# A fused linear-attention and token-mixing kernel: w spread by TensorE, decay by exponentials, tables and weights taken at other times, all orders searched anew

## The chip, the cores and the metric

The kernel runs on one core of one Trainium2 chip. The metric is device time in microseconds (us) of one execution. A verdict of faster or slower needs 2%. A run counts as slow when it is over 1.5% above the fastest run of the same kernel, and only fast runs are compared. Profiles are of one execution each, and their span is some 1.7 us shorter than the timed run's figure.

Engines in the profile: PE is TensorE (PEld its weight loads), DVE VectorE, ACT ScalarE, POOL GpSimd, SP SyncE, which here issues loads and stores. "L929" is a line of the kernel's file. A trailing q (SPq) is an engine's instruction queue.

## The reference, cut to what matters

```python
def _attn_ref(r, k, v, w, u):                 # r, k, v: 4 x 8 x 768 x 48; w, u: 8 x 48
    for t in range(S):
        cur = einsum('bhd,bhe->bhde', u * kt, vt)
        y[:, :, t] = einsum('bhd,bhde->bhe', rt, state + cur)
        state = w * state + einsum('bhd,bhe->bhde', kt, vt)

def _moe_ref(x, w_theta, w_tok_r, w_tok_i, w_ch):   # x: 4 x 768 x 384, the y of above
    theta = x @ w_theta
    zr, zi = x * cos(theta), x * sin(theta)
    u = x + w_tok_r @ zr + w_tok_i @ zi             # over the tokens
    return u + maximum(u @ w_ch, 0)
```

The kernel takes 256 tokens at a time (a pair of chunks of 128). The decay w becomes powers of w: r is scaled by w^t and k by w^-t, so that the recurrence turns into matrix products. The powers are `exp(t * ln w)`, made once on ScalarE, and everything else waits for them.

## The kernel before

The kernel is a list of tasks. Each task has an engine, a planned duration, the names that it reads (`rd`) and writes (`wr`), and a priority. A planner puts them in order with a table of tuned priorities, and they are then emitted in that order. Two things of it matter below. First, dependencies come from the order in which tasks are *added*:

```python
def add(self, opts, fn, rd=(), wr=(), prio=0.0, ...):
    # ... cut
    for k in rd:
        if k in self.writer:
            deps.add(self.writer[k])        # read after write
    for k in wr:
        if k in self.writer:
            deps.add(self.writer[k])
        deps.update(self.readers.get(k, ()))  # write after read
```

A task that reads a name before any writer of it has been added doesn't wait for the writer. It is the writer, added later, that waits for it. Second, where the planner expects TensorE to idle, it puts filler: two matmuls of zeros each, 100 such pairs.

```python
def warm(e):
    for _ in range(2):
        nc.tensor.matmul(bank("warm")[:, :C], zeros, zeros, start=True, stop=True, ...)
```

The start that the change rewrites:

```python
# w to all 128 partitions in one load, ln of it, six tables of powers
nc.scalar.dma_start(out=w_all, in_=...)               # the row repeated 128 times
P.add({ACT: act_op(HD)}, lambda e: nc.scalar.activation(
    bank("w")[:, :HD], w_all, Act.Ln), rd=["table", "w_all"], ...)
# ... six Exp: wpow x2, wpinvj x2, wpinv x2
P.add({ACT: (1280, 0)}, lambda e: nc.scalar.preload_act_table_set("trig_and_small"),
      rd=[(t, n) for t in ("wpow", "wpinv", "wpinvj") for n in range(2)],
      wr=["tables done"], prio=-186, name="trig")
# ... wup = w and u by partition, transposed on TensorE
def power(e):                                          # w ** 256, by squaring
    for i in range(REF.bit_length() - 1):
        nc.vector.tensor_mul(wR, *[wR if i else wup[:, :HP]] * 2)
P.add({DVE: (8 * 75, 142)}, power, rd=["wup"], wr=["wR"], prio=-100)
# ... wS = wR spread, on VectorE
```

Of the kernel before, what the change touches and what calls it, by code (L numbers as in the profile page):

```python
# [27 lines left out]
    0: (-1896, 4), 1: (-2763, 4), 2: (-4995, 2), 3: (-3601, 2), 4: (-2443, 2), 5: (-1397, 2), 6:  # L28
    (-3159, 16), 7: (-2942, 16), 8: (-3463, 8), 9: (-3515, 2), 10: (-1403, 8), 11: (-2193, 2), 12:
    (-3435, 8), 13: (-681, 8), 14: (-937, 8), 15: (2071, 8), 16: (1103, 4), 17: (-619, 4), 18:  # L30
    (-926, 4), 19: (-4791, 4), 20: (-2748, 4), 21: (-3667, 4), 22: (-771, 4), 23: (-754, 4), 24:
    (-1822, 1), 25: (-1861, 2), 26: (2175, 2), 27: (-4, 2), 28: (-2, 2), 129: (-1155, 16), 130:
    (-4315, 4), 131: (-1061, 16), 132: (-2753, 4), 133: (-2053, 16), 134: (-1978, 16), 135:
    (-3238, 16), 136: (-3891, 8), 137: (-4590, 1), 138: (-3333, 4), 139: (-4189, 8), 140: (-5295,
    1), 141: (-4754, 4), 142: (-3834, 12), 143: (-2711, 1), 144: (-2685, 4), 145: (-4467, 1), 146:
    (-4690, 2), 147: (-2495, 1), 148: (-4276, 2), 149: (-842, 2), 150: (-2017, 1), 151: (-2622,
    2), 152: (-1180, 8), 153: (-3428, 1), 154: (-4163, 4), 155: (-3120, 1), 156: (-5116, 2), 157:
    (-94, 1), 158: (1961, 1), 159: (1825, 2), 160: (-1058, 1), 161: (215, 2), 162: (263, 1), 163:
    (1029, 4), 164: (-378, 4), 165: (-96, 2), 166: (858, 8), 167: (-1833, 16), 168: (-1750, 16),
    169: (-1556, 16), 170: (-621, 10), 171: (-655, 1), 172: (3105, 4), 173: (2182, 2), 174: (2622,  # L40
    1), 175: (-569, 4), 176: (1579, 12), 177: (2292, 1), 178: (233, 4), 179: (1643, 1), 180: (339,
    2), 181: (809, 1), 182: (4670, 2), 183: (1450, 2), 184: (1167, 1), 185: (2345, 6), 186: (-114,
    8), 187: (1042, 1), 188: (2242, 4), 189: (-581, 1), 190: (532, 2), 191: (2385, 1), 192: (1695,
    1), 193: (822, 2), 194: (-853, 1), 195: (-1349, 2), 196: (-240, 1), 197: (2674, 4), 198: (789,
    4), 199: (-2387, 2), 200: (-74, 8), 201: (-1619, 16), 202: (-1567, 16), 203: (-1103, 16), 204:
    (-1330, 8), 205: (-400, 1), 206: (-29, 4), 207: (1699, 2), 208: (2535, 1), 209: (793, 4), 210:
    (2521, 12), 211: (3075, 1), 212: (392, 6), 213: (1782, 1), 214: (958, 2), 215: (2441, 1), 216:
    (1197, 2), 217: (924, 2), 218: (-921, 1), 219: (861, 2), 220: (1383, 8), 221: (1810, 1), 222:
    (1772, 2), 223: (-1328, 1), 224: (-1335, 1), 225: (-330, 2), 226: (-3469, 1), 227: (358, 2),
    228: (-3341, 1), 229: (-1638, 4), 230: (-1248, 4), 231: (-1246, 2), 232: (-588, 8), 233:  # L50
    (-1217, 16), 234: (-835, 4), 235: (-2791, 1), 236: (-486, 4), 237: (-1096, 16), 238: (-635,
    4), 239: (-2397, 1), 240: (-273, 6), 241: (-1017, 16), 242: (-621, 8), 243: (-2952, 1), 244:
    (-1704, 6), 245: (-994, 16), 246: (-2200, 12), 247: (-3308, 1), 248: (-816, 2), 249: (-829,
    16), 250: (-2428, 4), 251: (-3835, 1), 252: (-2176, 4), 253: (-681, 16), 254: (-2655, 4), 255:
    (-4721, 1), 256: (-1118, 2), 257: (-1043, 16), 258: (-1015, 16), 259: (-935, 16), 260: (-1828,
    16), 261: (-1011, 16), 262: (793, 8), 263: (909, 1), 264: (-33, 4), 265: (1341, 8), 266: (-71,
    1), 267: (380, 2), 268: (229, 12), 269: (-1257, 1), 270: (-362, 2), 271: (-3268, 1), 272:
    (265, 2), 273: (601, 2), 274: (-1105, 1), 275: (251, 4), 276: (-1692, 8), 277: (784, 1), 278:
    (69, 4), 279: (-1813, 1), 280: (-632, 2), 281: (-2190, 1), 282: (-3799, 1), 283: (-1835, 2),
    284: (-3289, 1), 285: (-2993, 4), 286: (-2547, 1), 287: (-1541, 4), 288: (-2225, 4), 289:  # L60
    (-2974, 2), 290: (-4026, 8), 291: (-887, 16), 292: (-1726, 8), 293: (-3616, 1), 294: (669, 6),
    295: (-588, 16), 296: (-1662, 12), 297: (-1938, 1), 298: (-362, 2), 299: (-639, 16), 300:
    (1192, 8), 301: (-3068, 1), 302: (13, 4), 303: (-1228, 16), 304: (-351, 12), 305: (-2932, 1),
    306: (-1642, 2), 307: (-871, 16), 308: (-323, 12), 309: (-4673, 1), 310: (-2831, 4), 311:
    (-664, 16), 312: (-2302, 4), 313: (-4826, 1), 314: (178, 2), 315: (-633, 16), 316: (-1135, 4),
    317: (-385, 16), 318: (-1248, 4), 319: (-789, 16), 320: (-655, 16), 321: (-631, 16), 322:
    (-481, 16), 323: (-815, 16), 324: (400, 8), 325: (-1810, 1), 326: (-1751, 4), 327: (-3166, 8),
    328: (-2789, 1), 329: (-3217, 6), 330: (-4693, 12), 331: (-3955, 1), 332: (-5497, 2), 333:
    (-4006, 1), 334: (-2820, 2), 335: (-900, 2), 336: (-1916, 1), 337: (-1250, 2), 338: (-1478,
    8), 339: (-3240, 1), 340: (-3478, 2), 341: (-3355, 1), 342: (-1715, 2), 343: (-1485, 1), 344:  # L70
    (-3363, 1), 345: (-1582, 2), 346: (-2081, 1), 347: (160, 2), 348: (-2004, 1), 349: (-689, 4),
    350: (-420, 4), 351: (-1725, 2), 352: (-1969, 8), 353: (-1341, 16), 354: (-1303, 16), 355:
    (-1238, 16), 356: (-1289, 16), 357: (-1210, 16), 358: (-3381, 8), 359: (-2762, 1), 360:
    (-2524, 4), 361: (-2830, 8), 362: (-3386, 1), 363: (-2897, 4), 364: (-4632, 4), 365: (-2013,
    1), 366: (-849, 2), 367: (-523, 1), 368: (1139, 2), 369: (-3189, 2), 370: (-3513, 1), 371:
    (-136, 2), 372: (-267, 8), 373: (1251, 1), 374: (-1229, 6), 375: (2164, 1), 376: (942, 1),
    377: (-3734, 2), 378: (472, 1), 379: (-932, 6), 380: (-2042, 1), 381: (1568, 4), 382: (-1352,
    4), 383: (244, 2), 384: (591, 8), 385: (-1168, 1), 386: (961, 1), 387: (677, 1), 388: (1888,
    1), 389: (-234, 1), 390: (-667, 1), 391: (-2365, 2), 392: (777, 1), 393: (-998, 1), 394:
    (-1886, 1), 395: (-3010, 1), 396: (-2471, 1), 397: (-3265, 1), 398: (-2463, 2), 399: (-1584,  # L80
    1), 400: (5, 4), 401: (-611, 1), 402: (-2652, 2), 404: (1045, 1), 405: (-2138, 1), 406:
    (-1323, 1), 407: (-2353, 1), 408: (-3333, 1), 409: (-1347, 1), 410: (-466, 2), 411: (1541, 1),
    412: (-902, 1), 413: (-1133, 1), 414: (-530, 1), 415: (1936, 1), 416: (-134, 1), 417: (768,
    2), 418: (-2718, 1), 419: (1200, 4), 420: (-1242, 1), 421: (-420, 2), 423: (-2297, 1), 424:
    (1071, 1), 425: (723, 1), 426: (2291, 1), 427: (92, 1), 428: (1298, 1), 429: (2134, 2), 430:
    (-582, 1), 431: (-1329, 1), 432: (-1371, 1), 433: (209, 1), 434: (-1462, 1), 435: (-4595, 1),
    436: (-1376, 2), 437: (-219, 1), 438: (-565, 6), 439: (-2142, 1), 440: (795, 2), 442: (-1207,
    16), 443: (-1191, 16), 444: (-970, 16), 445: (-929, 16), 446: (-1092, 16), 447: (556, 8), 448:
    (1415, 1), 449: (924, 4), 450: (829, 8), 451: (-178, 1), 452: (-1305, 6), 453: (682, 8), 454:
    (222, 1), 455: (-2254, 2), 456: (474, 1), 457: (174, 2), 458: (-34, 2), 459: (-2544, 1), 460:  # L90
    (-914, 2), 461: (303, 8), 462: (676, 1), 463: (-391, 4), 464: (-444, 1), 465: (-2364, 2), 466:
    (-1246, 1), 467: (-515, 1), 468: (-3108, 2), 469: (373, 16), 470: (-2049, 1), 471: (-2310, 4),
    472: (-2144, 4), 473: (-4193, 2), 474: (-1119, 8), 475: (-896, 16), 476: (-1250, 16), 477:
    (-740, 16), 478: (-677, 16), 479: (-1314, 16), 480: (804, 8), 481: (764, 1), 482: (-3469, 4),
    483: (-2213, 8), 484: (-507, 1), 485: (-3583, 6), 486: (-2024, 4), 487: (-2611, 1), 488:
    (-4241, 2), 489: (-5630, 1), 490: (-4793, 2), 491: (-3160, 2), 492: (-3117, 1), 493: (-425,
    4), 494: (-941, 8), 495: (786, 1), 496: (-1076, 2), 497: (-1758, 1), 498: (-561, 2), 499:
    (-636, 1), 500: (-1124, 1), 501: (1106, 2), 502: (2312, 16), 503: (-1559, 1), 504: (-936, 4),
# [228 lines left out]
def act_op(n, psum=True, ptr=False):  # L327
    return (n / 1.2 + (50 if psum else 100) + (90 if ptr else 0), 175)
# [40 lines left out]
def build(ctx, tc, nc, r, k, v, w, u, moe_w_theta, moe_w_tok_r, moe_w_tok_i, moe_w_ch, out):  # L369
    B, H, S, D = r.shape  # L370
    HD = H * D
# [609 lines left out]
```

## Time and profile before

| | before |
|---|---|
| median of 3 timed runs | 144.17 us (144.04 to 144.65) |
| the run that was profiled | 145.99 us, span 144.3 us, mean granted clock 0.976 |
| TensorE busy | 133.4 us, 17.4 of it filler |
| table loads of ScalarE | 2 |

Note the second row: the profile was taken on a run slower than the three timed ones. This comes back below.

The prediction shows most of the lines. One view it treats as unimportant is the end. These are the DMA throughput in GB/s of before in its last 7 us (40 slices of 0.175 us), and SyncE's waits in its last 10 us (who waits at which line, for what, total us, times, longest).

```profile
GB/s 298 325 395 386 334 404 9 0 0 0 0 0 0 0 0 0 0 0 97 369 395 360 360 386 343 378 395 334 386 351 325 18 0 0 0 0 0 0 0 0
```

```profile
SPq L976 <- DMA out_dram<-fin: 1.7, 1, 1.7
```

The last stores move at over 300 GB/s and stop dead, eight slices (1.4 us) before the end. SyncE's final wait for them is 1.7 us.

### The profile page before, as it was taken

To read this page: it belongs to the slowest core of one execution; us is meant where nothing else is said; L and a number is where in the kernel's file an instruction comes from. 1 tells how busy PE (TensorE), PEld (TensorE's weight loads), DVE (VectorE), ACT (ScalarE), POOL (GpSimd) and SP (SyncE) were. 2 spreads that over 40 slices of the span, in tenths; PEclk is the share of its full clock that TensorE was granted. 3 is DMA by queue.
4 is the path that set the end of the run, shared out by engine and by line. 5 is a ranking of instruction groups with operands and counts; after the bars stand their busy time and mean duration, and the time that the engine had idled before them with its cause. 6 is when DMAs were issued, how large, how long until landed. Compare 5 with 4: busy or idle time off the path is not lost.

```text
span 144.3 us, 3966 instructions
## 1 busy us (share of the span) xinstructions
PE 133.4 (92%) x1643; PEld 96.4 (67%) x1643; DVE 107.9 (75%) x161; ACT 76.0 (53%) x110; POOL 85.5 (59%) x74
## 2 busy tenths in 40 slices
PE   6628999999999999999999999998999999999970
PEld 6517988868978877667766776755666766666530
DVE  4288889994949597789759997768997987237451
ACT  3788368768778666474472575664049203700020
POOL 7475661459969548858959987993874404530000
PEclk9996599999999999999999999999999999999999
DMA  1999951999998989779999489869967377403935
GB/s 57 279 262 261 342 166 29 299 251 293 333 303 236 309 165 225 169 184 237 255 233 222 91 176 178 163 152 296 192 128 134 88 109 204 130 0 67 156 119 208
DMA packets 72586, 27.79 MB, mean 193 GB/s; under 512 B 67064, under 2 KB 71032, under 8 KB 72568
## 3 DMA queue, kind: packets, MB, share of 16 engines
q1 hardware_dynamic: 72424, 27.34, 79.7%
q8 instruction: 13, 0.21, 0.6%
q10 hardware_dynamic: 144, 0.20, 0.4%
q14 instruction: 5, 0.04, 0.1%
HBM read 20.25 MB, written 4.72 MB: 173 GB/s over the span
## 4 chain that ended last, share of the span: by engine, by line
PE 78%; DMA 8%; DVE 4%; ACT 3%; POOL 3%; issue 1%; DVEq 0%
PE bank L886 28%; PE bank L628 10%; PE bank L855 8%; PE bank L911 6%; PE bank L929 6%; PE bank L726 5%; PE bank L784 3%; DMA xT<-x 3%; PE bank L829 3%; PE bank L612 3%; DMA uT<-un 3%; DMA w_all<-in_w_dram 3%; PE bank L824 2%; PE bank L753 2%; POOL Kw L678 1%; POOL Rw L665 1%
## 5 line engine op out<-in xcount | busy, mean ns | idle before, releaser
L886 PE MATMUL bank<-zr,WrT 128*128 128x384 bf16 x144 | 34.5, 326 | 0.0
L886 PE MATMUL bank<-zi,WiT 128*128 128x384 bf16 x144 | 34.5, 326 | 0.0
L731 DVE TENSOR_TENSOR mAT<-bank,mask 128x1024 bf16<-128x1024 f32 x24 | 28.9, 1218 | 3.8 <-PE bank L726 3.7
L760 POOL TENSOR_TENSOR yd<-dg,vb 128x768 bf16<-128x768 f32 x12 | 17.7, 1474 | 15.9 <-ACT vb L401 6.8
L868 POOL TENSOR_TENSOR zi<-x,sin 128x768 bf16<-128x768 bf16 x12 | 19.7, 1639 | 12.4 <-ACT sin L859 12.4
L665 POOL TENSOR_TENSOR Rw<-ld,wpow 128x768 bf16<-128x768 f32 x11 | 20.0, 1815 | 8.5 <-DMA ld<-in_r_dram 5.6
L929 PE MATMUL bank<-zeros 128*128 128x128 bf16 x200 | 17.4, 239 | 1.2 <-DVE zeros L475 1.2
L859 ACT ACTIVATE sin<-bank 128x768 bf16<-128x768 f32 x12 | 9.7, 810 | 16.5 <-PE bank L855 7.9
L886 PEld LDWEIGHTS <-WiT 128*128 128x128 bf16 x144 | 12.8, 98 | 6.6
L886 PEld LDWEIGHTS <-WrT 128*128 128x128 bf16 x144 | 12.6, 97 | 6.6
L681 POOL TENSOR_TENSOR Kw<-ld,wpinv 128x768 bf16<-128x768 f32 x9 | 16.4, 1818 | 0.9 <-DMA ld<-in_k_dram 0.9
L916 DVE SCALAR_TENSOR_TENSOR fin<-bank,un 128x768 f32<-128x768 f32 (+1 forms) x13 | 11.6, 896 | 6.9 <-PE bank L911 6.9
L401 ACT ACTIVATE RT<-bank 128x1024 bf16<-128x1024 bf16 x12 | 12.3, 1022 | 8.2 <-PE bank L628 7.3
L929 PEld LDWEIGHTS <-zeros 128*128 128x128 bf16 x200 | 13.9, 108 | 2.6 <-DVE zeros L475 1.2
L894 DVE TENSOR_TENSOR un<-bank,x 128x384 bf16<-128x384 f32 x24 | 12.8, 552 | 3.2 <-PE bank L886 3.0
L401 ACT ACTIVATE KT<-bank 128x1024 bf16<-128x1024 bf16 x9 | 9.2, 1024 | 10.7 <-PE bank L628 10.7
L865 DVE TENSOR_TENSOR zr<-bank,x 128x768 bf16<-128x768 f32 x12 | 11.4, 953 | 4.4 <-ACT bank L862 4.4
L838 DVE TENSOR_TENSOR x<-bank,yd 128x768 bf16<-128x768 f32 x12 | 11.4, 953 | 4.0 <-PE bank L829 2.3
L911 PE MATMUL bank<-Wch,uT 128*128 128x384 bf16 x72 | 13.7, 326 | 0.7 <-ACT uT L401 0.4
L855 PE MATMUL bank<-Wth,xT 128*128 128x384 bf16 x72 | 13.7, 326 | 0.6 <-DMA xT<-x 0.6
L911 PEld LDWEIGHTS <-uT 128*128 128x128 bf16 x72 | 6.8, 98 | 5.5 <-DMA uT<-un 0.6
L862 ACT ACTIVATE bank<-bank,pi 128x768 f32<-128x768 f32 x12 | 10.5, 872 | 0.0
(93 smaller groups left out, 216.5 us busy)
## 6 DMA issues: line engine op xcount, KB each, us to landing
ld<-in_r_dram SPq DMA_DIRECT2D x12, 384.0 KB, 6.0
out_dram<-fin SPq DMA_DIRECT2D x11, 384.0 KB, 2.8
ld<-in_v_dram SPq DMA_DIRECT2D x18, 192.0 KB, 4.0
ld<-in_k_dram SPq DMA_DIRECT2D x18, 192.0 KB, 3.7
ld<-in_moe_w_tok_r_dram SPq DMA_DIRECT2D x6, 384.0 KB, 5.0
ld<-in_moe_w_tok_i_dram SPq DMA_DIRECT2D x6, 384.0 KB, 5.5
ld<-in_v_dram SPq DMA_DIRECT2D x3, 384.0 KB, 6.2
ld<-in_k_dram SPq DMA_DIRECT2D x3, 384.0 KB, 5.8
```

Source lines behind the costliest of these rows:

```text
L401: nc.scalar.activation(dst, src, Act.Copy)
L628: nc.tensor.matmul(bank16(tok)[:, i * C:(i + 1) * C], s, ident, is_transpose=True, start=(i == 0), stop=(i == n - 1))
L665: P.add(mul(g, 2.15), lambda e: eng_of[e].tensor_mul(Rw[:, :, :, :D].transpose([0, 2, 1, 3]), Ls[ir].rearrange("p (h n d) -> p h n d", h=H ...
L681: eng_of[e].tensor_mul(Kw[:, :, :, :D].rearrange("p a h d -> p (a h) d"), Ls[ik].rearrange("p (a d) -> p a d", d=D), wpinv.rearrange("p a ...
L731: P.add({DVE: dve_op(8 * C)}, lambda e, tk=tk, c=c: nc.vector.tensor_mul(mAT[:, c].rearrange("p a h t -> p (a h) t"), dbl(tk).rearrange("p ...
L760: P.add({POOL: pool_op(2 * HD, 1.7)}, lambda e: eng_of[e].tensor_mul(yd.rearrange("p a (h d) -> p (a h) d", h=H), wide(dg, D), vb.rearrang ...
L855: nc.tensor.matmul(dbl(th)[:, t, :HD], xT[:, ND * t + dk, :], Wth[:, dk, :], start=(dk == 0), stop=(dk == ND - 1))
L868: P.add({POOL: pool_op(2 * HD, 1.9)}, lambda e: eng_of[e].tensor_mul(zi[:, 2 * pr:2 * pr + 2], x[:, 2 * pr:2 * pr + 2], sn), rd=xk + [("si ...
L886: nc.tensor.matmul(bank(tm)[:, :HD], WT[:, so, to * C:(to + 1) * C], z[:, so], start=(so == 0 and part == 0), stop=(part == 2 * NP - 1 and ...
L894: P.add({DVE: dve_op(HD)}, lambda e, tm=tm, t=t, to=to: nc.vector.tensor_add(un[:, t], bank(tm)[:, :HD], x[:, to]), use=[tm], rd=[("x", zj ...
L911: nc.tensor.matmul(dbl(tf)[:, t - lo, :HD], uT[:, ND * t + dk, :], Wch[:, dk, :], start=(dk == 0), stop=(dk == ND - 1))
L929: nc.tensor.matmul(bank("warm")[:, :C], zeros, zeros, start=True, stop=True, skip_group_check=True)
```

## The change

Intent: get the powers of w earlier, take work off VectorE before its full stretch, and let the first loads of r, k and v go first. Then all orders were searched again by the planner. The core of the diff (the table of tuned priorities, which changes nearly every order, is cut):

```diff
-            nc.scalar.dma_start(out=w_all, in_=dataclasses.replace(
-                row, ap=[[0, C]] + [list(x) for x in row.ap[1:]]))
+            nc.scalar.dma_start(out=w_row, in_=w.rearrange("(o h) d -> o (h d)", o=1))
...
-        load(100, wu[:HP, :, :D], w.rearrange("(a b) d -> a b d", b=2), ["wu"], "u")
-        load(100, wu[HP:, :, :D], u.rearrange("(a b) d -> a b d", b=2), ["wu"], "u")
+        def wu_load(e):                      # the same two loads, on ScalarE's queue
...
+        P.add({PE: pe_op(850)}, lambda e: nc.tensor.matmul(
+            bank("w")[:, :HD], ones, w_row, start=True, stop=True),
+            rd=["ones", "w_row"], wr=["wlog"], acq=[("w", 1)], prio=-200)
...
         P.add({ACT: (1280, 0)}, lambda e: nc.scalar.preload_act_table_set("trig_and_small"),
-              rd=[(t, n) for t in ("wpow", "wpinv", "wpinvj") for n in range(2)],
-              wr=["tables done"], prio=-186, name="trig")
+              rd=[(t, n) for t in ("wpow", "wpinv", "wpinvj") for n in range(2)] + ["wR"],
+              wr=["tables done"], prio=9, name="trig")
...
-        def power(e):
-            for i in range(REF.bit_length() - 1):
-                nc.vector.tensor_mul(wR, *[wR if i else wup[:, :HP]] * 2)
-        P.add({DVE: (8 * 75, 142)}, power, rd=["wup"], wr=["wR"], prio=-100)
+        P.add({ACT: (100, 135)}, lambda e: nc.scalar.activation(lw_p, wup[:, :HP], Act.Ln),
+              rd=["wup", "table"], wr=["lw_p"], prio=-187)
+        P.add({ACT: (100, 135)}, lambda e: nc.scalar.activation(wR, lw_p, Act.Exp,
+                                                                scale=float(REF)),
+              rd=["lw_p"], wr=["wR"], prio=-186)
...
-        P.add({DVE: dve_op(HP * 2 * D)}, lambda e: nc.vector.tensor_mul(
+        P.add({POOL: pool_op(HP * 2 * D, 1.9)}, lambda e: nc.gpsimd.tensor_mul(
             wS, wide(wR, 2 * D), bc(bmask, 1, HP)), rd=["wR", "bmask"], wr=["wS"], prio=-100)
...
-            rd=L2(i) + ["tables done"], wr=[(key, o)], prio=prio)
+            rd=L2(i), wr=[(key, o)], prio=prio)
...
-            P.add({PE: (115, 217)}, warm, rd=["zeros"], ...
+            P.add({PE: (115, 217)}, warm, rd=["zeros", "wlog"], ...
```

Look at `"wR"` in the fourth hunk. It is in the list of names that the load of the sine table reads, but the task that writes wR is added below it.

## The prediction

> **What bounds the kernel now.** I read the page first (tenths by slice and the chain that ended last), then the timeline of the first 36 us, then the waits, then the windows of the filler matmuls. The page says that TensorE is the limit over most of the span.
>
> ```profile
> PE 133.4 (92%) x1643; PEld 96.4 (67%) x1643; DVE 107.9 (75%) x161; ACT 76.0 (53%) x110; POOL 85.5 (59%) x74
> ...
> PE   6628999999999999999999999998999999999970
> ...
> PEclk9996599999999999999999999999999999999999
> ...
> PE 78%; DMA 8%; DVE 4%; ACT 3%; POOL 3%; issue 1%; DVEq 0%
> ...
> L929 PE MATMUL bank<-zeros 128*128 128x128 bf16 x200 | 17.4, 239 | 1.2 <-DVE zeros L475 1.2
> ```
>
> The reader is to see two things. TensorE is full from slice 3 on, but 17.4 of its 133.4 us are line 929: matmuls of zeros, put in by the order where it expected TensorE to idle. So "full" is not "bound". And the granted clock falls to 0.5 to 0.6 in slices 3 and 4 (10.8 to 18 us), when the first real work runs.
>
> The windows of line 929 place the filler: 3.6 us in 0 to 5, 1.5 in 5 to 10, and 12.3 us from 10 to 57, at about a third of TensorE's time in 20 to 30; none after 57. Thus three stages: a start (0 to 12), a starved stage (12 to 57), and a stage of full real matmuls (57 to 138.5) with a tail of 5.8 us.
>
> The timeline of the start carries the argument:
>
> ```profile
> 0.83 0.40 ACTq L461 DMA_DIRECT2D w_all<-in_w_dram  x1
> ...
> 1.32 0.83 SPq L455 DMA_DIRECT2D wu<-in_w_dram  x1
> ...
> 2.20 0.63 SPq L455 DMA_DIRECT2D wu<-in_u_dram  x1
> ...
> 4.62 0.49 ACT L523 ACTIVATE bank<-w_all 128x384 f32<-128x384 f32 x1 [2.54 <-DMA w_all<-in_w_dram]
> ...
> 7.48 0.61 ACT L528 ACTIVATE wpow<-bank,tok_f 128x384 f32<-128x384 f32 x1
> ...
> 8.11 1.28 ACT L532 ACT_TABLE_LOAD   x1
> 8.17 1.81 POOL L665 TENSOR_TENSOR Rw<-ld,wpow 128x768 bf16<-128x768 f32 x1 [2.90 <-ACT wpow L528]
> 8.34 2.05 DVE L552 TENSOR_TENSOR wS<-wR,bmask 128x384 f32<-128x384 f32 x1
> ...
> 10.57 2.30 DVE L665 TENSOR_TENSOR Rw<-ld,wpow 128x768 bf16<-128x768 f32 x1 [0.18 <-DMA ld<-in_r_dram]
> ...
> 12.12 1.03 PE L628 MATMUL bank<-ident,Kw 128*128 128x128 bf16 x8 [0.55 <-POOL Kw L678]
> ```
>
> The chain that ended last begins with exactly these: the spread load of w (3.76 us), its Ln, six exponentials of 0.47 us apart, then r's scaling and k's scaling on GpSimd, one after the other, then the flip of Kw at 12.12. GpSimd had sat 2.90 us waiting for the last power table; r's data was there.
>
> In the starved stage VectorE is the nearest limit first (5.00 of 5.00 us busy in 20 to 25 and in 25 to 30), and the loads next. The load queue stands still behind one load of v that needs a buffer:
>
> ```profile
> SPq L455 <- DMA ld<-in_moe_w_theta_dram: 5.1, 1, 5.1
> SPq L455 <- ACT Wth L401: 3.9, 1, 3.9
> ```
>
> That load was issued only at about 23.6, after ScalarE had got round to converting w_theta (22.79). In 20 to 25 the core moved 18 GB/s against 262 to 328 in the ten us before: a hole of some 4.5 us in which about 1.2 MB could have come. Later GpSimd waits 5.6 us in four places for r and 3.1 for v.
>
> **What the Trainium skill says.** (1) "TensorE: Matmul & The Clock Gate", section "What's actually happening": an idle window of about 3.4 us halves the array's clock, a busy one restores it. The trace agrees: fillers at 6.12 run 24 in 1.51 us (63 ns each), then TensorE idles from 7.6 to 10.3, and at 12.12 eight flips take 1.03 us (128 ns), at 19.33 0.61 us. (2) "DMA: Bandwidth & Descriptors", section "Anatomy of one DMA": a fixed cost of about 2.0 us and then bytes; it is stated for another issue path, but here the 192 KB stores landed in 2.0 us, so a 1.5 KB row should need about that, not w_all's 3.76. (3) "FP8 and Floating Point Precision", section "TensorE Precision Notes": a true fp32 matmul takes four passes; no fp32 matmul of this size is in this trace. (4) "ScalarE: Activation LUTs", section "What ACT_TABLE_LOAD costs": 1283 ns for a load; the trace shows 1.28.
>
> **The change part by part.**
>
> *w as one row, spread by TensorE.* Removes a 192 KB read by all partitions, adds one fp32 matmul of ones by the row. Landing: 0.83 + 2.0 = 2.85. Matmul: a cold filler takes 3.59/32 = 0.112 us for 128 columns, so 384 columns in four passes are 3 x 4 x 0.112 = 1.35: done at 4.3 with a little latency. Ln until 4.9. So Ln is no earlier than before, at best 0.3: by itself this part is worth almost nothing in latency. It frees 0.2 MB of DMA, 0.75 us at 270 GB/s, in which r's and k's data come.
>
> *Order of the exponentials.* Only the two wpow tables stand before r's scaling, the two wpinv are sent behind the first pairs: wpow ready at 4.9 + 2 x 0.47 = 5.85 instead of 8.09. Gain 2.25 us. wpinvj at 6.8.
>
> *First scalings.* The new table puts r's first scaling on VectorE (0.95 us alone) and k's on GpSimd (1.81): flips of Rw from 6.9, of Kw from about 8.7 instead of 12.12. Gain 3.4 us if r and k are there. r, then k, then v are now first in the queue, and the 1.46 us of wu's two issues have left it, so they should be in by 4 to 6 us.
>
> *Decay by exponentials, wS on GpSimd.* Removes eight products on VectorE (0.16 + 1.34 us) and wS (2.05, slowed by GpSimd's Rw beside it; the other product of 384 on VectorE takes 0.55). Adds two tiny ScalarE instructions and a GpSimd product, about 0.9 us, when nothing waits for it: wS is first read at 17.5 now. VectorE so gets 3.5 us back just before its full stretch, and pays 0.95 for Rw.
>
> *wu on ScalarE's queue.* Costs ScalarE some 1.4 us of issuing from 2.1 to 3.5, while it waits for w anyway: hidden. Moves all loads 1.4 us forward.
>
> *Table of sines later, and no wait of the conversions on it.* The 1.28 us leave 8.11 to 9.39, in front of v's conversion and w_theta's; they return before the first sine (31.35 now). ScalarE is 53% busy: hidden. The useful part is that w_theta's conversion is no longer pinned, and in the new table the second load of w_theta is eighth and the load that reuses the first one's buffer lies some nine loads after it, not three: the hole after 18 us should shrink.
>
> *Fillers wait for the row's product.* TensorE starts with that matmul at 2.9 and then fills without a break from 4.3 to the first flips at 7; the idle 7.6 to 10.3 is gone, so the clock should be full by about 8 to 10 and stay. Now some 5 us of real work at 12.1 to 18.5 run at half speed: up to 2.5 us, of which I count half.
>
> *Sum.* Weights are 3.4 us earlier, data 1.4 to 2.1 us earlier, VectorE's stretch some 3 us. Whichever of the three ends last sets the shift: I take 2.3. Clock: 1.2. Less filler through the smaller hole: 12.3 us are to be had at most; I take 0.8, since a new order can lose elsewhere what it gains here. Full stage and tail: unchanged, its operations are the same. 144.2 - 4.3 = **139.9 us**, said as 140.0.
>
> **The rivals.** (a) *The loads are the real clock of 12 to 57.* For it: VectorE waited for r at 10.57 and GpSimd at 13.65 (1.58 us); DMA tenths of 9 throughout. Then only the earlier start and the 0.2 MB count, 1.4 to 2 us: 142.3, and "same". Against: VectorE full in 20 to 30 while DMA stood still. (b) *The hole closes wholly and fillers vanish.* For it: 4.5 us of dead DMA and 12.3 us of filler. Then 4 more us: 136. Against: VectorE's own work is 108 us and would be next. (c) *The new wait: the fp32 matmul.* If the row comes at 3.3 and the product takes 2 us, Ln is at 5.4, and the gain in tables falls to 1.7: 140.8. (d) *A new stall by the new order:* orders are fixed beforehand, the measured waits differ from the planned, as the hole shows; a load held for a buffer elsewhere could cost 2 to 4 us and leave 143 to 144. (e) *TensorE bound wholly, nothing of the start matters:* ruled out by the filler.
>
> **Range and chances.** 2% is 2.9 us: under 141.3. (a) and (d) lie above it, (b), (c) and the middle below. I give (a) and (d) together 0.3, of which 0.03 for slower by over 2%. Range 137.2 (half of b) to 142.6 (a with a bit of d).
>
> **What would show it.** The matmul of ones in the timeline at 2.9 to 4.3; Ln by 4.9; the first Rw by 6; the first flip of Kw at about 9; granted clock full by slice 3; filler after 10 us at or under 10 us; no SyncE wait of over 4 us for w_theta; the stage after the last filler to the end unchanged, about 87 us. Wrong it would be if the first Rw waits for r rather than for wpow, if the clock is low again in slices 3 and 4, or if DMA shows another empty slice before 57.

## The result, and the profile after

| | before | after |
|---|---|---|
| median | 144.41 us (4 runs, 144.04 to 145.67) | 149.70 us (4 runs, 148.95 to 150.36) |
| profiled span | 144.3 us | 147.2 us |
| mean granted clock of the profiled run | 0.976 | 0.965 |
| table loads | 2 | 5 |

The ratio of fast runs is 1.0349, with a 95% interval of 1.0267 to 1.0431: slower. Ratios here and below are the mean time of one kernel's fast runs over the mean of the other's fast runs of the same rounds, so they aren't quite the ratios of the medians quoted beside them. Sent again later as a control (label c_after, chip 2), the changed kernel took 150.18 us against 145.44, ratio 1.0416 (1.0368 to 1.0463). Expected there:

> The changed kernel itself, as a control on the same chip as the next three: 1.03 to 1.04 of the kernel before.

The page of after, first the busy times, then tenths by slice of 3.7 us for TensorE and its granted clock, and last the largest group of filler matmuls:

```profile
PE 137.0 (93%) x1645; PEld 98.5 (67%) x1645; DVE 103.4 (70%) x151; ACT 77.2 (52%) x109; POOL 88.4 (60%) x78
...
PE   3968599999999999999999999799999999999991
...
PEclk9995559999999999999999999999999999999999
...
PE 78%; ACT 8%; DMA 7%; DVE 2%; issue 1%; SPq 1%; ACTq 0%
...
L939 PE MATMUL bank<-zeros 128*128 128x128 bf16 x200 | 17.6, 242 | 0.0
```

VectorE did lose 4.5 us of work. TensorE isn't fuller in the start, and its recorded half clock lasts from slice 3 to 5 (11.2 to 21.5 us) instead of 3 to 4. In the chain that ended last, ScalarE has gone from 3% to 8%.

A caution for all that follows: this line, and the mean granted clock, count the clock as full until the trace's first clock record. In both kernels the matmuls of 128 columns start 107 ns apart until that record (4.7 us in before, 7.8 in after), as they do in the recorded half-clock stretch, and 56 ns apart at full clock. So the array is slow from the beginning too, and a mean clock of 1.000 doesn't say that it wasn't.

The timeline of the start says why the gain is missing (start, duration, engine, line, what; in brackets the idle time before it and what ended it):

```profile
2.22 1.61 PE L527 MATMUL bank<-w_row,ones 1*128 1x384 f32 x2 [2.22 <-DVE bmask L473]
...
3.87 0.47 ACT L530 ACTIVATE bank<-bank 128x384 f32<-128x384 f32 x1 [1.24 <-PE bank L527]
...
5.57 0.96 DVE L675 TENSOR_TENSOR Rw<-ld,wpow 128x768 bf16<-128x768 f32 x1 [0.62 <-ACT wpow L536]
...
9.02 0.61 PE L638 MATMUL bank<-ident,Kw 128*128 128x128 bf16 x8
...
9.90 1.28 ACT L541 ACT_TABLE_LOAD   x1
...
11.20 1.02 ACT L402 ACTIVATE KT<-bank 128x1024 bf16<-128x1024 bf16 x1
12.24 1.28 ACT L551 ACT_TABLE_LOAD   x1
...
13.53 0.20 ACT L551 ACTIVATE lw_p<-wup 128x4 f32<-128x4 f32 x1
13.76 1.28 ACT L553 ACT_TABLE_LOAD   x1
15.05 0.20 ACT L553 ACTIVATE wR<-lw_p 128x4 f32<-128x4 f32 x1
15.16 1.01 ACT L402 ACTIVATE RT<-bank 128x1024 bf16<-128x1024 bf16 x1
15.33 0.83 POOL L562 TENSOR_TENSOR wS<-wR,bmask 128x384 f32<-128x384 f32 x1 [6.96 <-ACT wR L553]
...
16.22 0.35 PE L763 MATMUL bank<-uw,PD 128*128 128x2 bf16 x8 [1.94 <-ACT RT L402]
```

Until 9.02 us everything goes as intended; the flip of k (transpose by TensorE) was at 12.12 before. Then three table loads stand between ScalarE's evictions, back to back with them. The sine set comes at 9.90. It throws out the set with logarithm and exponential, which lw_p and wR still need, so the compiler put a load ahead of each, and a fifth ahead of the first sine (28.99). The second eviction of RT comes at 15.16, later than before's 14.91, although the first one came at 8.87 instead of 11.54. TensorE idles 1.94 us for it (last line).

The plan says the same: its task for wR depends on the sine load, not the other way round. That is the rule of `add` shown above. (lw_p doesn't depend on it; its input is planned for 10.6 us, and the sine load, with nothing to wait for but the six tables, for 9.5.) The planner counted lw_p and wR at 100 ns each, for it doesn't know of loads that the compiler adds.

Now the end of after: throughput in the last 7 us, the instruction packets in it (queue and kind: packets, MB, share), then SyncE's last wait.

```profile
GB/s 0 0 0 0 0 0 0 0 246 351 413 369 325 377 316 386 360 384 351 342 228 0 0 9 9 9 18 26 18 26 26 0 0 0 0 0 0 0 0 0
...
q8 instruction: 1, 0.02, 0.9%
```

```profile
SPq L986 <- DMA out_dram<-fin: 3.3, 1, 3.3
```

The store doesn't stop dead. It trickles at 9 to 26 GB/s for another 1.4 us, and SyncE waits 3.3 us instead of 1.7. In the packets of the trace, a 16,384-byte packet of instructions runs from 143.34 us for 960 ns. The trace doesn't name the DMA engine of a packet, but each engine closes its part of a store with a packet of 4 bytes: 15 of the last store's 16 are done by 143.94, and the 16th comes at 145.65, behind 16 data packets that start one by one from 144.29, when the instruction packet ends. So one engine held the store up. At that time TensorE runs 44 filler matmuls that the new order has left behind its last real one (141.55 to 144.17).

### The profile page after: what moved, and what is told of

Same layout as the page of the kernel before. It is cut to its first block, busy times and chain, and to the rows that moved or that the text cites. A ratio compares the mean times of both kernels' runs of the same rounds, so it can differ in the third digit from the quotient of the medians.

```text
span 147.2 us, 3972 instructions
## 1 busy us (share of the span) xinstructions
PE 137.0 (93%) x1645; PEld 98.5 (67%) x1645; DVE 103.4 (70%) x151; ACT 77.2 (52%) x109; POOL 88.4 (60%) x78
## 4 chain that ended last, share of the span: by engine, by line
PE 78%; ACT 8%; DMA 7%; DVE 2%; issue 1%; SPq 1%; ACTq 0%
PE bank L896 30%; PE bank L638 8%; PE bank L921 8%; DMA ld<-in_v_dram 7%; PE bank L939 7%; PE bank L865 7%; PE bank L736 4%; PE bank L794 3%; PE bank L839 3%; PE bank L622 3%; PE bank L834 2%; PE bank L763 1%; ACT RT L402 1%; PE bank L802 1%; ACT L553 1%
## 5 line engine op out<-in xcount | busy, mean ns | idle before, releaser
L675 POOL TENSOR_TENSOR Rw<-ld,wpow 128x768 bf16<-128x768 f32 x10 | 19.1, 1916 | 1.5 <-DMA ld<-in_r_dram 1.5
L402 ACT ACTIVATE RT<-bank 128x1024 bf16<-128x1024 bf16 x12 | 12.3, 1021 | 7.7 <-PE bank L638 7.6
L926 DVE SCALAR_TENSOR_TENSOR fin<-bank,un 128x768 f32<-128x768 f32 (+1 forms) x13 | 11.6, 895 | 6.5 <-PE bank L921 6.5
L402 ACT ACTIVATE KT<-bank 128x1024 bf16<-128x1024 bf16 x8 | 8.2, 1020 | 5.0 <-PE bank L638 5.0
```

The costliest lines, as they stand in the source:

```text
L402: nc.scalar.activation(dst, src, Act.Copy)
L675: P.add(mul(g, 2.15), lambda e: eng_of[e].tensor_mul(Rw[:, :, :, :D].transpose([0, 2, 1, 3]), Ls[ir].rearrange("p (h n d) -> p h n d", h=H ...
```

## The experiments

Two suspects: the table loads, and the trailing filler. A third question stays even when both are gone: why the good start isn't worth 4 us. Fourteen kernels ran, the control among them, in four batches on four chips (5, 2, 6 and 1). Each is compared with runs of before on its own chip; a comparison of two kernels by their ratios can thus be one across chips. By the 2% rule after and c_after are slower, e2, e3 and e4 are unclear, and all others are the same as before.

| label | edit in short | ratio to before (95%) |
|---|---|---|
| after / c_after | the change | 1.0349 / 1.0416 |
| e1_no_reload | after, no early sine load | 1.0027 (0.9988 to 1.0066) |
| e2_no_tail_fill | after, no trailing filler | 1.0201 (1.0163 to 1.0239) |
| e5_no_reload_no_fill | both | 0.9957 (0.9918 to 0.9996) |
| e3_before_3_loads | before, three more table loads | 1.0154 (1.0089 to 1.0220) |
| e4_before_new_start | before's order, the new start | 0.9867 (0.9775 to 0.9958) |
| e6_and_loads_later | e5, some loads issued later | 0.9911 (0.9872 to 0.9950) |
| e7_before_start_no_hole | e4, one load issued later | 0.9878 (0.9835 to 0.9920) |
| e8_before_no_mid_fill | before, no filler after 10 us | 1.0016 (0.9976 to 1.0056) |
| e9_new_start_no_mid_fill | e7, no filler after 10 us | 0.9883 (0.9843 to 0.9922) |
| e10_before_tail_fill | before, 44 trailing fillers | 1.0025 (0.9981 to 1.0069) |
| e11_new_order_no_mid_fill | e6, no filler after 10 us | 0.9878 (0.9840 to 0.9915) |
| e12_tail_fill_with_fetch | e10, 27 filler pairs fewer in the middle | 1.0053 (1.0015 to 1.0091) |
| e13_tail_fill_no_fetch | e1, 27 filler pairs fewer in the middle | 0.9908 (0.9882 to 0.9935) |

All gave correct results.

### The table loads: e1_no_reload and e3_before_3_loads

e1 is the changed kernel without the task that loads the sine set; all orders stay. The compiler then loads it ahead of the first sine.

```diff
     for t in P.order():
-        t.fn(t.eng)
+        if t.name != "trig":
+            t.fn(t.eng)
```

> The changed kernel, every order kept, without its early load of the sine tables; so Ln and Exp of the decay find their table still there, and three of the five table loads (9.90, 12.24, 13.76 us, 1.28 each) are gone; the one in front of the first sine stays. Theory A (the decay's exponentials pay table loads, they hold ScalarE's evictions and so the first pairs): 2.5 to 4 us less than the changed kernel's 149.7, so 145.5 to 147. Theory B (the loss is in the new order further on, in loads held for buffers, and in the tail): within 1 us of 149.7.

Measured: 146.2 us median against 145.18, ratio 1.0027. The timeline of e1 at the same place:

```profile
10.50 1.02 ACT L403 ACTIVATE KT<-bank 128x1024 bf16<-128x1024 bf16 x1 [0.50 <-PE bank L639]
11.42 0.20 ACT L552 ACTIVATE lw_p<-wup 128x4 f32<-128x4 f32 x1
11.65 0.20 ACT L554 ACTIVATE wR<-lw_p 128x4 f32<-128x4 f32 x1
11.76 1.01 ACT L403 ACTIVATE RT<-bank 128x1024 bf16<-128x1024 bf16 x1
```

lw_p and wR follow each other in 0.2 us each with no load between: the first set does hold both functions. The second eviction of RT is at 11.76 instead of 15.16, and only two table loads are left (1.37 and 24.69). Since after stood at 1.035 to 1.042, the loads cost 3.2 to 3.9%, or 4.6 to 5.6 us (estimate: these shares of 144.4). The ratio leaves out five of e1's twelve runs (147.1 to 147.9 us) as slow; by the medians of all runs the loads cost 2.6 to 3.0%, or 3.7 to 4.3 us (estimate: 1.033 and 1.037 against 1.007). Three times 1.28 us is 3.84, so anything from none to 1.8 us is left over. The clock would fit as the rest: in the profile of after full clock returns only at 21.47 us, at the end of 3.41 us without idle time of TensorE, the first such stretch after its 1.94 us wait for RT; in e1's profile full clock comes at 12.80, also after such a stretch (9.38 to 12.80). But these are two single profiles, and no run separates the two parts.

e3 is the opposite: before with the two log and exponential sets loaded after its first eviction of KT, so that the compiler adds a third load ahead of the first sine.

```diff
     for t in P.order():
         t.fn(t.eng)
+        if t.seq == 141:
+            nc.scalar.preload_act_table_set("natural_log_exp_and_others")
+            nc.scalar.preload_act_table_set("exp_and_others")
```

> The kernel before with three table loads more, two behind the first eviction of KT (some 14 us) and one in front of the first sine, as the changed kernel has them; no other change, same results. Theory A: 2 to 4 us more than before (146.5 to 148.5). Theory B (ScalarE has slack, loads are hidden): within 1 us of before.

Measured: 147.59 us against 145.18, ratio 1.0154, so some 2.2 us. Loads of this kind do move the end, in the other kernel too. By how much may depend on what stands behind them: in after TensorE waited 1.94 us for the delayed RT, in e3 1.27 us for a delayed Sb (17.36 us). That is a reading of two profiles, not a test.

### The trailing filler: e2_no_tail_fill and e5_no_reload_no_fill

e2 drops the 28 pairs that after plans behind 130 us; e5 does what e1 and e2 do.

```diff
     for t in P.order():
-        t.fn(t.eng)
+        if not (t.name == "warm" and t.start > 130000.0):
+            t.fn(t.eng)
```

> The changed kernel without the 28 pairs of filler matmuls that its order puts behind the last real matmuls (140 us on); nothing else moved. Theory T (the fillers, or the fetch of their instructions beside the last stores, hold the end; the tail from the last channel matmul to the end was 5.65 us against 3.9 before): 1 to 2 us less, about 148. Theory not-T (the end is the landing of the last store, whatever TensorE does): within 0.5 us of 149.7.

> The changed kernel without the early sine table (as e1) and without the 28 filler pairs at the end (as e2). If the two costs are apart and add up (table loads 1.0349 to 1.0027, tail 1.0349 to 1.0201 of before): 0.985 to 0.992 of the kernel before, and some 4.5% under the changed kernel. If they overlap: about 1.00.

Measured: e2 147.77 us, ratio 1.0201, last wait of SyncE 1.6 us and no instruction packet in the last 7 us. e5 143.9 us, ratio 0.9957. On the same chip, c_after stood at 1.0416, so both edits together are worth 4.6 points. They account for all of the loss: what is left is level with before, or barely better. They don't account for the missing gain.

### Was it the filler? e10_before_tail_fill

If matmuls of zeros behind the end cost time as such, they must cost it in before too. Here 44 of them follow its last real matmul, into a PSUM bank that is free by then.

```diff
     for t in order:
         t.fn(t.eng)
+    for _ in range(44):
+        nc.tensor.matmul(P.bankset[spare][:, 0][:, :128], P.zeros, P.zeros, ...)
```

> The kernel before with 44 filler matmuls (the same as the changed kernel's last group) added behind TensorE's last real matmul, into a bank that is free by then. Theory T (trailing fillers lengthen the end, by the fetch of instructions that the last store meets): slower than before by 1.0 to 2.0%, some 146.5 to 148 us, SyncE's last wait for the store over 2.5 us instead of 1.7. Rival (the long tail came with the new order's last stores, and taking the fillers out helped for another reason): ratio within 0.5% of 1.

Measured: 145.4 us against 145.3, ratio 1.0025, and the last wait of SyncE:

```profile
SPq L983 <- DMA out_dram<-fin: 1.7, 1, 1.7
```

My theory in the form that the expectation has it fell: the filler costs nothing here. But there was no instruction packet in this tail either. In before's trace the 16 KB packets come at every 95 to 155 matmuls, and the last one at matmul 1610 in before and in e10 alike. So where it falls depends on how many instructions TensorE has had, not on the filler at the end.

### The packet alone: e12_tail_fill_with_fetch and e13_tail_fill_no_fetch

e12 adds the same 44 to before and drops 27 filler pairs from the middle, which moves the last packet 54 matmuls on. e13 does this to e1, where it should push the packet behind the end, with the trailing filler left in.

```diff
+    mid = [t.seq for t in order if t.name == "warm" and t.start > 10000.0]
     for t in order:
-        t.fn(t.eng)
+        if t.seq not in mid[-27:]:
+            t.fn(t.eng)
```

> The kernel before with the same 44 filler matmuls behind the last real one, and 27 filler pairs fewer in the middle, which cost nothing in the runs without any. The 16 KB instruction packets come every 110 to 150 matmuls (estimate from the trace: the last at matmul 1626 of 1662), so 54 matmuls fewer should move the last one to about matmul 1680 of the old count, some 18 fillers behind the last real matmul, in the middle of the last store. Theory P (the packet, not the fillers): an instruction packet after the last real matmul, the last wait for the store 2.5 to 3.3 us instead of 1.7, ratio to before 1.006 to 1.015. Rival (another trait of the new order makes the long tail): the packet is there and the last wait stays at 1.6 to 1.8 us, ratio within 0.5% of 1.

> The changed kernel's order without the second table loads and with its trailing fillers (measured at 1.003 of before, last wait 3.3 us), with the last 27 filler pairs of the middle taken out, so that the 16 KB packet, which came at matmul 1651 of 1665, would come behind the last one. Theory P: no packet in the last store, the last wait 1.6 us although the 44 trailing matmuls are there, ratio to before 0.993 to 0.998, as when the trailing fillers were taken out (0.996). Rival (the fillers or the order): the wait stays at 3.3 us, ratio about 1.003.

The last 7 us of e12, throughput, instruction packets, and SyncE's wait:

```profile
GB/s 0 0 0 0 0 0 9 307 404 342 377 369 360 387 351 369 369 334 360 88 94 0 0 0 0 9 9 9 9 26 9 0 0 0 0 0 0 0 0 0
...
q8 instruction: 1, 0.02, 0.9%
```

```profile
SPq L985 <- DMA out_dram<-fin: 3.6, 1, 3.6
```

And of e13, which has the trailing filler and no packet there:

```profile
GB/s 351 386 114 0 0 0 0 0 0 0 0 0 0 0 0 0 0 0 176 369 342 413 360 342 378 360 377 325 369 369 307 9 0 0 0 0 0 0 0 0
```

```profile
SPq L989 <- DMA out_dram<-fin: 1.5, 1, 1.5
```

For the wait this settles it. Before now has after's trickle, and its last wait has gone from 1.7 to 3.6 us. The changed order has its filler and a clean end. In time, e12 stands at 1.0053, a little under the 1.006 to 1.015 that I expected (145.63 us; 0.3 points above e10, whose interval it overlaps). Its profile is of a run of 146.97 us, the second longest of its fast ones, so the 1.9 us of added wait need not be in every run. e13 stands at 0.9908, better than expected and 1.2 points under e1, which differs from it only by 27 filler pairs (and by the chip). Filler from the middle costs nothing (e8 below), so I put the 1.2 points to the packet, some 1.7 us. That its cost in time lies between 0.3 and 1.2 points is all that these pairs show. In before, then, its last packet at 134.6 us was good luck.

### The start alone: e4_before_new_start and e7_before_start_no_hole

e4 keeps before's orders and takes in the new start alone: the row and its product, wpow and wpinvj first, wu on ScalarE's queue, lw_p and wR while the first set is still loaded, wS on GpSimd, the sine set after the second eviction of RT.

```diff
-    for t in P.order():
-        t.fn(t.eng)
+    then = {0: [6, 7], 16: [17, 18, 21, 22, 19, 20], 25: [26], 139: [28], 172: [23]}
+    # tasks on the right are sent right behind the one on the left
...
-                nc.vector.tensor_mul(wR, *[wR if i else wup[:, :HP]] * 2)
+            nc.scalar.activation(lw_p, wup[:, :HP], Act.Ln)
+            nc.scalar.activation(wR, lw_p, Act.Exp, scale=float(REF))
```

> The order of the kernel before with the new start alone: w as a row and spread by TensorE, wpow first, wu on ScalarE's queue, decay by Ln and Exp while their table is still loaded, wS on GpSimd, sine table behind the second eviction of RT. Two table loads in all, as before. If the start's parts are worth what the prediction said and the loss is the new order and its reloads: 1.5 to 3.5 us less than before (141 to 143). If the early stage is bound by loads or by TensorE: within 1 us of before.

Measured: 144.34 us median of 4 runs, two of them slow; fast ones 143.97 and 142.05, ratio 0.9867. In the profile its lead over before was 3.1 us at 33 us and 1.0 at 57. A load held for a buffer seemed to eat it, so e7 sends that load five loads later (`258: [260]` added to the map).

> As e4 (order of before, new start), and the load of v that waits for w_theta's buffer from 13.2 to 21.3 us is issued six loads later. If the loads are the clock of 24 to 57 us: 1 to 3 us less than e4, so about 0.97 of before. If TensorE's queue with its fillers is the clock: within 0.7 us of e4 (0.987).

Measured: 142.47 us (142.02 to 142.91), ratio 0.9878. Each event below is the start of the first, third and so on of VectorE's twelve additions that make x (`x<-bank,yd`), and of its last output instruction:

| profile | 1st x | 3rd | 5th | 8th | 12th | last output |
|---|---|---|---|---|---|---|
| before (a run of 145.99) | 25.0 | 36.2 | 58.0 | 86.5 | 116.6 | 140.6 |
| e7 (a run of 142.91) | 21.6 | 31.9 | 54.6 | 83.1 | 113.1 | 137.5 |

With the hole closed, the lead of 3.4 us stays whole to the 12th x. In time e7 and e4 can't be told apart: e4 has only two fast runs, 1.9 us from each other, so whether the hole costs anything isn't shown. And the lead of the profiles isn't the gain: the profile of before is of a run of 145.99 us, above its three timed ones (144.04 to 144.65). The start is worth what the rounds say, 1.2%, about 1.7 us, and not the 3 that two single profiles suggest.

e7 is among the fastest kernels of the study (e4, e9, e11 and e13 can't be told from it): 1.2% under before and 5% under after. By the limit of 2% its class is "same".

### Loads in the new order: e6_and_loads_later

In after, SyncE stands 7.1 us behind a load of v that waits for GpSimd's Kw, and 5.3 us behind w_ch (2.4 for a landing of r and 2.9 for GpSimd's Rw). e6 is e5 with w_ch (and its conversion) and two loads of v sent later.

```diff
+    then = {247: [319], 248: [320], 357: [632, 633]}
```

> As e5, and the three loads that stood in the queue waiting for a buffer (w_ch at 17.1 to 21.4 us, two of v at 41.1 to 45.3 in e1) are issued a few loads later, where their buffers are long free. If the lead of 4 to 6 us, which e1 has at 20 to 45 us and has lost at 95 us, is lost to these holes in the loads: 1 to 3 us less than e5. If it is lost to TensorE's own queue (fillers, order): within 0.7 us of e5.

Measured: 143.45 us, ratio 0.9911. That is half a point under e5, with overlapping intervals. Its profiled run was slow (156.43 us, clock 0.838), so I read nothing from its trace.

### Do the fillers in the middle hold real work up? e8, e9 and e11

The 12.3 us of filler were a gain to be had in my sum. These three kernels drop every filler pair planned after 10 us: from before, from e7, and from e6.

```diff
-        t.fn(t.eng)
+        if not (t.name == "warm" and t.start > 10000.0):
+            t.fn(t.eng)
```

> The kernel before without its 71 pairs of filler matmuls planned after 10 us (12.3 us of TensorE in the trace between 10 and 57 us); nothing else is touched. Theory F (the fillers stand in TensorE's fixed order ahead of real work that is already there, so they eat time): the ratio to before falls by over 2%, 142 us or less, and TensorE stays busy without them. Theory M (they only cover idle time, in which TensorE would wait for the vector engines or the loads): the ratio stays within 0.5% of 1, and the idle time before TensorE's real matmuls between 10 and 57 us is about 12 us. Theory C (they hold the clock up): slower by over 0.5%, with the granted clock under 0.95 somewhere between 20 and 57 us.

> The kernel before with the new start and no load hole (measured at 0.988 of before), without the 71 filler pairs planned after 10 us. It asks what eats the lead of some 3 us that the new start has at 20 to 35 us. Theory F (fillers in TensorE's fixed order): the lead lasts to the end, ratio to before 0.975 or less, 141 us or less. Theory M (the lead is eaten by waits that the fillers cover: loads or vector engines): ratio 0.984 to 0.992 as with the fillers, and the lead of the milestones shrinks in the same places, with idle TensorE there. Theory C: ratio over 0.992, with a low granted clock.

> The changed kernel's order, without the second table loads, with the load of w_ch and two loads of v sent later (measured at 0.991 of before), without any filler planned after 10 us (87 pairs). Theory F: ratio to before 0.978 or less. Theory M: ratio 0.985 to 0.997, like with the fillers. Theory C: over 0.997, granted clock under 0.95 between 20 and 60 us.

Measured: 145.49 us (ratio 1.0016), 143.41 (0.9883) and 143.41 (0.9878). None of the three moved by half a point against its counterpart with filler. The windows of TensorE in before and then in e8 (stretch, its length, busy us and matmuls, granted clock, DMA share, GB/s):

```profile
10.00:20.00 10.00, 9.16 (x122) 0.66 1.17 295
20.00:30.00 10.00, 9.65 (x188) 1.00 0.56 162
30.00:40.00 10.00, 10.00 (x144) 1.00 1.06 285
40.00:57.00 17.00, 17.00 (x259) 1.00 0.98 250
```

```profile
10.00:20.00 10.00, 8.93 (x119) 0.66 1.17 295
20.00:30.00 10.00, 7.85 (x136) 0.91 0.73 196
30.00:40.00 10.00, 9.09 (x98) 0.92 1.00 288
40.00:57.00 17.00, 15.75 (x222) 1.00 0.97 240
```

TensorE's idle time in these 47 us is 5.4 us, against 1.2 in before. So the filler covers waiting; it doesn't cause it. Two of my numbers were off. I had expected about 12 us of idle time, but the records of matmuls overlap: counted from each start to the next, before's fillers hold TensorE for 9.6 us, not 12.3. And the clock did fall to 0.91 and 0.92 between 20 and 40 us, so the same work took longer there, by at most 1.7 us. This cost no time in the end either.

## Why the prediction was wrong, point by point

**Right.** The start itself came as written: the product of ones at 2.22 to 3.83 us (said: 2.9 to 4.3), the logarithm done at 4.34 (by 4.9), the first Rw at 5.57 (by 6), the flip of Kw at 9.02 (about 9). SyncE's wait for w_theta is gone. Rival (c), a slow fp32 product, didn't come: 1.61 us for both of its records together. It started 0.7 us earlier than I had it: the row, issued at 0.80, was there by 2.22 us, in at most 1.4 us; the 2.0 us of the prediction's second citation were, as it says, for another issue path.

**Wrong: the tables.** The step that failed is "two tiny ScalarE instructions [...] when nothing waits for it", and with it "ScalarE is 53% busy: hidden". I had noted that the sine load is moved later, and read `rd` + `"wR"` as "after wR". With the rule of `add` it means the reverse, because wR's writer is added below. So the kernel loads tables five times instead of twice, and three loads of 1.28 us stand between evictions that TensorE needed: 3.2 to 3.9% by fast runs, 2.6 to 3.0% by the medians of all. This was in the diff and in the source to be seen. The loads are the larger part of the loss. Rival (d), "a new stall by the new order", is nearest to it, but I had given slower by over 2% only 0.03. Two of the signs that I had named spoke against me as well: the clock low in slices 3 and 4, and filler after 10 us of 11.2 us up to 135 and 3.5 after it, not 10.

**Wrong: the end.** "Full stage and tail: unchanged, its operations are the same." The operations are; their count ahead of the end isn't, and a 16 KB instruction packet came to lie in the last store: 0.7 to 1.5 points by e1 against e5 and after against e2, 1.2 by e13 against e1, but only 0.3 by e12 against e10. No rival had it.

**Mis-sized: the gain of the start.** 2.3 for the shift, 1.2 for the clock and 0.8 for filler made 4.3. With both faults out and before's order kept, e7 has about 1.7 us for all three.
- The 0.8 us for filler is nothing: e8, e9 and e11 show that the filler hides waits.
- The 1.2 us for the clock came from one profile and from a mean clock that leaves the beginning out. Of before's 45 runs on chip 6, 21 had a mean clock of 0.99 or more, with a median of 144.82, and 24 had less, with 145.81; on chip 2 these two medians were 145.44 (17 runs) and 145.52 (14). That doesn't separate runs with a cold stretch from runs without: e10, with before's own start and a mean clock of 1.000, has its matmuls 107 ns apart until past 13.3 us. What the half clock costs isn't shown.
- The granted clock was to be full by 8 to 10 us and stay. In after it came at 7.8, but was half again from 11.2 for 10.24 us (in before's profile from 11.6 for 6.83). In the profiles of e1 and e5 it came only at 12.8 and 12.6; in those of e4 and e7, with before's order, at 9.6 and 7.1. There it stayed. So the step that bridged the gap with filler came true only in the last two, one profile each.
- The prediction's first citation says that the trace agrees. It does for the rates (63 and 128 ns a matmul), not for what halves the clock: before's idle stretch was 2.7 us, and in after the clock fell at 11.23 us although TensorE was busy for 1.86 of the 3.41 us before and never idle for more than 0.67. What halved it isn't shown here.
- Shift and clock together are then e7's 1.7 us, where I took 3.5. How they split isn't shown.

**The order.** With the same start and both faults out, the new order (e5, 0.9957) is some 0.8 points behind before's (e7, 0.9878). e6 and e11 come back to 0.9911 and 0.9878 with loads issued later, which speaks for the holes in the load queue that the search had moved to w_ch and v. But e6's interval overlaps e5's, and e13, with the new order, these holes and neither fault, has 0.9908 on its chip, against e5's 0.9957. So a loss by the new order of 0.3 to 0.8 points is likely, not shown.

**Open.** How the cost of the table loads splits into the loads themselves and the longer cold clock; why e12 lost only 0.3 points against e10 with 1.9 us more waiting in its trace (one long run, as said above); how e7's gain splits into shift and clock; and how large the new order's own loss is.

## What to carry to other kernels

When a change touches a dependency list, ask which task waits for which in the plan, not what the list seems to say, and count table loads in the new trace first: here two activations of 0.2 us, placed behind the load of another set, went with three loads more of 1.28 us. Take the base of a prediction from the timed runs; a single profile can be of a long run, its mean clock can leave the beginning out, and an idle stretch filled on purpose is no work to be saved. Look at the last store: if it trickles on one DMA engine, a few instructions more or less, anywhere before, can move what it met.

## What the Trainium skill lacked or had wrong

- "Runtime: NRT & Kernel Launch", section "Instruction fetch mechanics", says that blocks of 16 KiB are fetched by the sequencer's own DMA queue and that the cost is mostly hidden. The traces agree on the size (13 packets of 16,384 bytes in before), and the cost is hidden but for one place. A packet of 985 ns in the last store of e12 held one DMA engine back and lengthened SyncE's last wait from 1.7 to 3.6 us (e10 against e12). The page doesn't warn of this.
- "ScalarE: Activation LUTs", section "Table sets: the hidden batching unit", says that a logarithm and then an exponential need one load, since one set holds both. That holds when this set is loaded already (e1: no load between them). After the sine set, the compiler placed one load ahead of each (after: 12.24 and 13.76 us).
- The same page, section "What ACT_TABLE_LOAD costs", gives 1283 ns and a drain of about 1380 ns more. The load took 1.28 us here too, but no drain follows in the trace: the load at 9.90 ends at 11.18 and the next eviction starts at 11.20.
